# Block-recurrent cross attention and an ELU layer on one core: planner costs for loads and stores, longer runs for moved softmax weights, and two softmax steps on GpSimd

## The chip, the cores and the metric

The kernel runs on one core of a Trainium2 chip. The metric is the device time of one execution in microseconds, the median of the runs. Names: PE is the matrix engine (PEld its weight loads), DVE or VectorE the vector engine, ACT or ScalarE the scalar engine, POOL or GpSimd the fourth compute engine, SP the engine whose queue issues nearly all DMAs. SBUF and PSUM are the on-chip memories[...].

## The reference

```python
B, H, S, Ns, D = 8, 8, 512, 32, 64        # x: (B,H,S,D), state: (B,H,Ns,D)
scores = x @ state.T / sqrt(D);  a = softmax(scores)      # over the 32 states
xread  = a @ state                                        # (B,H,512,64)
scores2 = state @ x.T / sqrt(D); a2 = softmax(scores2)    # over the 512 rows
sread  = a2 @ x                                           # (B,H,32,64)
t = concat([xread, sread], axis=2)        # 544 rows per batch
t = t.transpose(0, 2, 1, 3).reshape(4352, 512)
h = t @ w_in                              # 512 -> 2048
g = where(h > 0, h, exp(min(h, 0)) - 1)   # ELU
out = g @ w_out                           # 2048 -> 512
```

All is in float32.

## The kernel before

**Work by batch.** The 512 x rows of a batch never pass through xread. The kernel multiplies the state of the batch with w_in first (`make_m`, four pieces, PSUM to the tiles m or s by ScalarE), so that the first layer is a product of these pieces with the softmax a, held transposed in the tile aT (`a_sb`). Both layers use a seven-product scheme (Strassen with Winograd's sums), so every product needs sums of blocks: the sums of the m pieces and of a_sb run on GpSimd (`sum_m`, `sum_a`), those of the second layer on VectorE (`Second.sums`, `combine`). sread is collected for all batches (`state_read`) and goes through both layers at the end (`states`).

**One batch in the steady loop** (`batch(b)`, b = 2 to 7):

- `load_blocks(b+1, ob)`: 16 DMAs of 64 KB bring the next x, in 128 B runs, into the tile o. The same tile holds the finished output rows of the batch before until `store` has written them out, so these loads follow the stores.
- The first layer: four chunks (`ffn1_chunk`) of seven products of two matmuls of 128x128 by 128x256. ScalarE and VectorE take each result from PSUM: copies into u2 and u3 (tile sec), additions back into PSUM (`ps<-sec,ps`), the ELU (`xe`, then `g`).
- `turn_blocks(ob, xr)`: four VectorE transposes in 32x32 blocks (`xr<-o`), one for each group of four block loads.
- The second layer (`ffn2`): one product of 16 pairs of matmuls, then six sub-products of seven steps each (`second[2]`, `[4]`, `[6]`, `[7]`, `[5]`, `[3]`). Each step's result is added to the output tile by VectorE (`o<-o,ps`). Near its start come `scores(b+1)` into two PSUM banks of their own (6 and 7) from xr.
- `soft_next()` inside `ffn2`, for the next batch: `softmax` (over states) into a_sb, `softmax_rows` (over rows), `load_x` (four DMAs of 256 KB into xe), `move_state` and then the GpSimd sums. a_sb is also scratch for the sums of `second[2]` and `second[6]`, so the new softmax can be written to it only when `second[6]` has been multiplied.
- `state_read(b+1)`, near the end of `ffn2`: needs xe and the moved weights.

**softmax(b, to)** for a half g, on tiles of 128x512: transpose from PSUM to xr (VectorE), maximum over 32 (VectorE), subtract it (`xr<-xr,small`), exp (ScalarE), sum (VectorE); then, for both halves, reciprocal (VectorE), multiply (`xr<-xr,small`), transpose into a_sb (VectorE). The subtraction and the multiplication have two tile operands. For b > 1 they are on VectorE, for b = 0 and 1 on GpSimd.

**move_state(b)**: two VectorE transposes put the row softmax back into the first half of xr, then 16 DMAs of 32 KB move it to the second half of xr, 32 partitions each, in 8 runs of 128 B per partition. `turn_state` does this for batches 0 and 1 by PE and a ScalarE copy.

**Order.** Every operation is recorded in a `Plan` with a cost; `Plan.order` runs a list scheduler over them three times and keeps the best order. All engines then execute their instructions in that order, each in its own. PE's operations are preferred in the order of the program, those of VectorE, ScalarE and SP by due time, GpSimd's stay in program order. For a DMA, `DMA_COST` gives the issue cost and the rate; the plan adds `LANDING` = 2.2 us. `plan.behind(op)` makes the operations recorded inside it (GpSimd's excepted) depend on `op` in the plan; it puts no wait into the program. In `ffn2` the list `late` collects such marks: `late[4]` is the last sum of `second[6].sums`, `late[6]` the last one of `second[7].sums`.

Because all instructions are emitted by one helper (line 463), the profile shows L463 everywhere; groups are told apart by tile names: xr<-o are `turn_blocks`, o<-in_x_dram `load_blocks`, xr<-xr DMAs `move_state`, aT `a_sb`.

Of the kernel before, what the change touches and what calls it, by code (L numbers as in the profile page):

```python
# [21 lines left out]
ENGINES = (POOL, PE, DVE, ACT, SP)  # L22
DMA_COST = {
    "load_w": (0.44, 285e3), "load_w4": (0.44, 370e3), "load_x": (0.6, 270e3), "load_states": (0.6, 75e3),
    "load_blocks": (0.66, 280e3), "move_state": (0.66, 280e3),
}


# [50 lines left out]
class Op:  # L79
    __slots__ = (  # L80
        "number", "engine", "cost", "emit", "deps", "opens", "closes", "port", "moved", "start",
        "end", "due", "users", "name", "instr", "shape", "rank", "rate", "turn", "nudge", "spare",
    )


class Plan:
# [51 lines left out]
    def add(self, engine, cost, emit, ins, outs, port=False, moved=0, tokens=((), ()), name="", shape=None):  # L138
        op = Op()
        op.number, op.engine, op.cost, op.emit = len(self.ops), engine, cost, emit  # L140
        op.deps, op.opens, op.closes, op.port, op.moved = set(), None, [], port, moved
        op.name, op.shape, op.rank, op.rate = name, shape, None, 350e3
        op.nudge, op.spare = 0.0, None
        pieces = []
        banks = {}
        for writes, aps in ((False, ins), (True, outs)):
            for a in aps:
                if isinstance(a, View):
                    banks[id(a.bank)] = a.bank
                else:  # L150
                    pieces.append((writes,) + self.region(a))
        for writes, names in enumerate(tokens):
            for t in names:
                self.writers.setdefault(t, [])
                self.readers.setdefault(t, [])
                pieces.append((bool(writes), t, 1))
        for writes, key, mask in pieces:
            if key is None:
                continue
            for m, o in self.writers[key]:  # L160
                if m & mask:
                    op.deps.add(o)
            if writes:
                for m, o in self.readers[key]:
                    if m & mask:
                        op.deps.add(o)
        for writes, key, mask in pieces:
            if key is None:
                continue
            if writes:  # L170
                self.writers[key] = [
                    (m & ~mask, o) for m, o in self.writers[key] if m & ~mask
                ] + [(mask, op)]
                self.readers[key] = [(m & ~mask, o) for m, o in self.readers[key] if m & ~mask]
            else:
                self.readers[key].append((mask, op))
        for b in banks.values():
            if b.last is None:
                b.first = op
            else:  # L180
                op.deps.add(b.last)
            b.last = op
        op.deps.discard(op)
        self.ops.append(op)
        return op
# [52 lines left out]
    def run(self, until=0.0):  # L238
# [68 lines left out]
        while len(done) < len(self.ops):  # L307
            best = None
            for e in ENGINES:
                found = pick(e)  # L310
                if found and (best is None or found[0] < best[0] - 1e-9):
                    best = found + (e,)
            assert best is not None, "no operation is ready"
            at, op, e = best
            if e == POOL:
                in_turn.pop(0)
            able[e].remove(((op.turn if e == PE else op.due), op.number, op))
            if e == PE:
                t = free_at[PE]
                while at < until and t + 0.5 < at:  # L320
                    free = [i for u, i in banks if u <= t]
                    if free:
                        fills.append((t, free[-1], 0))
                    elif spare:
                        fills.append((t, spare.index, 1))
                    t += 0.3
            for bank in self.opening.get(op, ()):
                t, i = got = choice(op)[0]
                banks.remove(got)
                bank.index = i  # L330
                if i in holder:
                    after.append((holder[i], op))
                opened.add(op)
            if op in self.kept:
                banks = [b for b in banks if b[1] != self.kept[op]]
                if self.kept[op] in holder:
                    after.append((holder[self.kept[op]], op))
            while oldest < len(openers) and openers[oldest] in opened:
                oldest += 1
            if e == PE and (op.spare or op.name == "make_m"):  # L340
                spare = op.spare
            if e == PE and op.shape != shape:
                at += self.TURN
                shape = op.shape
            op.start, op.end = at, at + op.cost
            free_at[e] = op.end
            if op.port:
                port, holds = op.end, e
            if op.moved:
                wire = max(wire, op.end) + op.moved / op.rate  # L350
                op.end = wire + self.LANDING
                lanes.append(op.end)
            done.append(op)
            for u in op.users:
                ready[u] = max(ready[u], op.end + self.lag(op, u))
                waiting[u] -= 1
                if not waiting[u]:
                    release(u)
            for b in self.closing.get(op, ()):
                bisect.insort(banks, (op.end + self.LAG[op.engine].get(PE, 0.0), b.index))  # L360
                holder[b.index] = op
# [27 lines left out]
def kernel(  # L389
# [154 lines left out]
    def dma(out, in_, tokens=((), ()), queue=SP, kind="dma"):  # L544
        size = 4 * elements(out) * out.shape[0]
        engine = nc.sync if queue == SP else nc.scalar
        cost, rate = DMA_COST.get(kind, (0.44, 370e3))
        op = plan.add(
            queue, cost, issue(engine, "dma_start", dict(out=out, in_=in_)), [in_], [out],
            moved=size, tokens=tokens, name=kind,  # L550
        )
        op.rate = rate

    def bank():
        return Bank(plan).view()
# [194 lines left out]
    def softmax(b, to):  # L750
# [7 lines left out]
            V.transpose(out=soft_t(b, g), in_=s[g])  # L758
        for g in range(G):
            V.reduce_max(out=tops(b, g)["top_t"], in_=rows(g), axis=AX_X)  # L760
            (V if 3 & 1 and b > 1 or b in [] else Q).tensor_tensor(
                out=rows(g), in0=rows(g), in1=bc(tops(b, g)["top_t"], NS), op=ALU.subtract
            )
            A.activation(out=soft_t(b, g), in_=soft_t(b, g), func=AF.Exp, scale=scale)
            V.reduce_sum(out=tops(b, g)["total_t"], in_=rows(g), axis=AX_X)
        V.tensor_scalar(out=total_t, in0=total_t, scalar1=eps, scalar2=None, op0=ALU.add)
        V.reciprocal(out=total_t, in_=total_t)
        for g in range(G):
            (V if 3 & 2 and b > 1 or b in [] else Q).tensor_tensor(
                out=rows(g), in0=rows(g), in1=bc(tops(b, g)["total_t"], NS), op=ALU.mult  # L770
            )
            V.transpose(out=to[:, g * 512 : (g + 1) * 512], in_=soft_t(b, g))

    def read_weights():
        return xr[:, 1024:].rearrange("p (g r q) -> p g r q", g=G, q=P)

    def turn_state(b):
        for g in range(G):
            ps = bank().rearrange("p (r q) -> p r q", r=R)
            a = soft_a(b, g).rearrange("p (r q) -> p r q", r=R)  # L780
            turns(0.6, [(ps[:, r], a[:, r], ident, {}) for r in range(R)], "turn_state")
            A.copy(out=read_weights()[:, g], in_=ps)

    def move_state(b):
        t = xr[:, :1024]
        for g in range(G):
            V.transpose(out=t[:, g * 512 : (g + 1) * 512], in_=soft_a(b, g))
        t_v = t.rearrange("p (g r q n) -> p g r q n", g=G, r=R, n=NS)
        for m in range(NP):
            for q in range(P // 32):  # L790
                dma(
                    read_weights()[q * 32 : (q + 1) * 32, :, :, m * NS : (m + 1) * NS],
                    t_v[m * 32 : (m + 1) * 32, :, :, q], kind="move_state",
                )

    def state_read(b, at=x_halves):
        ps = bank()
        calls = []
        for g in range(G):
            for r in range(R):  # L800
                for m in range(NP):
                    calls.append((
                        ps[m * NS : (m + 1) * NS, g * D : (g + 1) * D],
                        read_weights()[:, g, r, m * NS : (m + 1) * NS],
                        x_rows(at, r)[:, m * P + g * D : m * P + (g + 1) * D],
                        dict(start=r == 0, stop=r == R - 1, tile_position=(0, m * NS)),
                    ))
# [260 lines left out]
    def store(b, h, o):  # L1068
        rows = out_b[b, 0:S].rearrange("(p r) c -> p r c", r=R)
        dma(rows[:, 2 * h : 2 * h + 2], o.o_sb[h], kind="store")  # L1070

    def words(raw):
        return [raw.rearrange("p n (j w) -> p n j w", w=2)[:, :, :, i] for i in range(2)]
# [196 lines left out]
    def ffn2(o, b):  # L1270
# [42 lines left out]

        def soft_next():
            if nxt:
                with plan.behind(late[4]):
                    softmax(b + 1, a_sb)
                    softmax_rows(b + 1)
                    load_x(b + 1, x_halves)
# [297 lines left out]
```

## Time and profile before

| | |
|---|---|
| median of 3 runs | 712.54 us (711.35 to 713.09) |
| the profiled execution | 712.58 us, span 710.7 us |
| PE busy | 695.2 us, 98% |
| VectorE busy | 584.5 us, 82% |
| ScalarE busy | 304.9 us, 43% |
| GpSimd busy | 113.8 us, 16% |
| DMA | 132771 packets, 78.54 MB; 113760 packets under 512 B |

The span is the time from the first to the last instruction of one profiled execution; the time of an execution includes about 1.9 us around it. Matmuls overlap and the profile models their ends, so stalls of PE are better read from the distance between the starts of consecutive matmuls: 0.216 us for 128x128 by 128x256 in an unbroken row, 0.112 us for 128x128 by 128x128. A bracket at the end of a timeline row is the engine's idle time before it and what ended it.

### The profile page before, as it was taken

What the parts mean: (1) busy time and instruction counts of PE and PEld (TensorE: products, weight loads), DVE (VectorE), ACT (ScalarE), POOL (GpSimd) and SP (SyncE); (2) the same over time, 40 slices, a digit from 0 to 9 for tenths busy, and PEclk for the clock granted to TensorE, in tenths of its full rate; (3) what the DMA queues carried; (4) which work ended last, traced back from release to release, by engine and by line L of the source; (5) the groups of instructions that cost most, each with busy time, mean ns of one, the idle gap of its engine ahead of it and who ended that gap; (6) DMA issues with size and microseconds to landing.
All of it is one profiled execution on the core that took longest, in us unless ns stands there. A gap on an engine that the chain in (4) does not pass through costs nothing.

```text
span 710.7 us, 14531 instructions
## 1 busy us (share of the span) xinstructions
PE 695.2 (98%) x5802; PEld 589.9 (83%) x5802; DVE 584.5 (82%) x1039; ACT 304.9 (43%) x604; POOL 113.8 (16%) x137
## 2 busy tenths in 40 slices
PE   8899999999999999999999999999999999999996
PEld 7544478889978998789877997799878988899995
DVE  4989999999659996799679994899579976997640
ACT  4989981011066124731275124712374127500630
POOL 1400000022230034100710063002510063000000
PEclk9999999999999999999999999999999999999999
DMA  9677772214270416550482326340664035200300
GB/s 221 197 265 244 272 241 44 59 36 114 90 193 15 120 32 187 110 119 2 93 231 64 61 50 187 91 120 3 186 141 115 5 64 205 60 1 31 119 8 24
DMA packets 132771, 78.54 MB, mean 111 GB/s; under 512 B 113760, under 2 KB 114272, under 8 KB 132704
## 3 DMA queue, kind: packets, MB, share of 16 engines
q1 hardware_dynamic: 130492, 77.06, 39.6%
q8 instruction: 46, 0.75, 0.4%
q10 hardware_dynamic: 2212, 0.56, 0.4%
q14 instruction: 21, 0.17, 0.1%
HBM read 61.34 MB, written 13.11 MB: 105 GB/s over the span
## 4 chain that ended last, share of the span: by engine, by line
PE 82%; DMA 6%; SPq 5%; ACT 2%; DVE 2%; issue 1%; ACTq 0%; DVEq 0%
PE ps L463 82%; SPq L463 5%; DMA w_in_mem<-w_half 2%; DMA o<-in_x_dram 2%; DMA out_dram<-o 1%; DVE g L463 1%; ACT sec L463 1%; DMA xe<-in_x_dram 1%; DMA g<-in_x_dram 1%; DVE ps L463 1%; ACT w_half L463 0%; ACT xe L463 0%; DVE xr L463 0%; ACT o L463 0%; ACTq L463 0%
## 5 line engine op out<-in xcount | busy, mean ns | idle before, releaser
L463 PE MATMUL ps<-aT,m 128*128 128x256 f32 (+1 forms) x568 | 151.2, 408 | 3.6 <-DVE ps L463 1.3
L463 PE MATMUL ps<-w_out,g 128*128 128x128 f32 (+1 forms) x864 | 143.5, 314 | 0.0
L463 PEld LDWEIGHTS ps<-w_out,g 128*128 128x128 f32 x864 | 126.3, 191 | 12.7 <-issue 4.2
L463 PEld LDWEIGHTS ps<-aT,m 128*128 128x128 f32 x568 | 104.2, 190 | 35.7 <-issue 15.9
L463 DVE TENSOR_TENSOR o<-o,ps 128x128 f32<-128x128 f32 (+2 forms) x239 | 67.4, 283 | 43.1 <-PE ps L463 41.5
L463 ACT COPY o<-ps 128x128 f32<-128x128 f32 (+2 forms) x70 | 23.1, 335 | 170.3 <-PE ps L463 164.3
L463 POOL TENSOR_TENSOR m<-m 128x256 f32<-128x256 f32 x72 | 65.9, 939 | 76.6 <-ACT m L463 75.2
L463 POOL TENSOR_TENSOR aT<-aT 128x256 f32<-128x256 f32 x24 | 17.9, 767 | 361.6 <-DVE aT L463 361.2
L463 PE MATMUL ps<-sec 128*128 128x128 f32 x560 | 74.8, 276 | 0.0
L463 ACT ACTIVATE xe<-ps 128x512 f32<-128x512 f32 x96 | 56.2, 597 | 38.5 <-DVE ps L463 21.5
L463 PEld LDWEIGHTS ps<-sec 128*128 128x128 f32 x560 | 68.1, 192 | 2.6 <-DVE sec L463 2.1
L463 PE MATMUL ps<-t_w,s 128*128 128x128 f32 (+1 forms) x432 | 64.7, 299 | 0.0
L463 PEld LDWEIGHTS ps<-t_w,s 128*128 128x128 f32 x432 | 58.4, 192 | 3.7 <-ACT m L463 0.8
L463 DVE SCALAR_TENSOR_TENSOR g<-xe,ps 128x512 f32<-128x512 f32 x66 | 43.9, 681 | 16.2 <-ACT xe L463 16.0
L463 ACT COPY m<-ps 128x512 f32<-128x512 f32 (+1 forms) x56 | 27.1, 534 | 59.6 <-PE ps L463 59.6
L463 PE MATMUL ps<-aT,s 128*128 128x256 f32 x168 | 41.8, 383 | 2.6 <-DVE ps L463 2.4
L463 ACT COPY sec<-ps 128x512 f32<-128x512 f32 (+1 forms) x52 | 29.6, 570 | 30.9 <-PE ps L463 17.4
L463 ACT ACTIVATE xe<-xe 128x512 f32<-128x512 f32 x66 | 40.7, 632 | 1.2
L463 PEld LDWEIGHTS ps<-aT,s 128*128 128x128 f32 x168 | 31.2, 190 | 9.4 <-DVE ps L463 4.0
L463 PE MATMUL ps<-w_half,kT 64*32 64x256 f32 x1024 | 35.9, 382 | 1.5 <-DVE w_half L463 0.9
L463 DVE TENSOR_TENSOR ps<-sec,ps 128x512 f32<-128x512 f32 (+1 forms) x52 | 34.7, 667 | 2.0 <-ACT sec L463 1.0
L463 ACT COPY ps<-ps 128x512 f32<-128x512 f32 (+1 forms) x28 | 15.3, 547 | 45.7 <-PE ps L463 45.7
(152 smaller groups left out, 1147.0 us busy)
## 6 DMA issues: line engine op xcount, KB each, us to landing
w_half<-w_in_mem SPq DMA_DIRECT2D x54, 512.0 KB
t_w<-in_moe_w_out_dram SPq DMA_DIRECT2D x8, 1024.0 KB
t_w<-in_moe_w_in_dram SPq DMA_DIRECT2D x7, 1024.0 KB
out_dram<-o SPq DMA_DIRECT2D x14, 512.0 KB
xe<-in_x_dram SPq DMA_DIRECT2D x26, 256.0 KB
o<-in_x_dram SPq DMA_DIRECT2D x80, 64.0 KB
w_in_mem<-w_half SPq DMA_DIRECT2D x8, 512.0 KB
xr<-xr SPq DMA_DIRECT2D x96, 32.0 KB
```

The lines of the kernel that those rows point to most:

```text
L463: ins = getattr(engine, name)(**named)
```

## The change

Four things are changed.

1. Costs in the planner: a block load lands 1.5 us later in the plan (field `wait`), and a store has its own rate of 200e3 bytes per us where the default was 370e3.
2. `softmax`: the subtraction and the multiplication go to GpSimd for every batch.
3. The state weights: their place in xr is ordered by (m, g, r, n), so that each of the 16 DMAs of `move_state` moves one run of 1 KB per partition; the transposes in front of them and the copies of `turn_state` write to strided places, and `state_read` reads the new order. The amounts are the same.
4. `soft_next` is planned behind `late[6]`.

The line `nudge = 0` sets the value that is there already.

```diff
 DMA_COST = {
 ...
-    "load_blocks": (0.66, 280e3), "move_state": (0.66, 280e3),
+    "load_blocks": (0.66, 280e3, 1.5), "move_state": (0.66, 280e3),
+    "store": (0.44, 200e3),
 }
...
                 wire = max(wire, op.end) + op.moved / op.rate
-                op.end = wire + self.LANDING
+                op.end = wire + self.LANDING + op.wait
...
-        cost, rate = DMA_COST.get(kind, (0.44, 370e3))
+        cost, rate, *wait = DMA_COST.get(kind, (0.44, 370e3))
...
-        op.rate = rate
+        op.rate, op.wait = rate, sum(wait)
...
-            (V if 3 & 1 and b > 1 or b in [] else Q).tensor_tensor(
+            (V if 0 & 1 and b > 1 or b in [] else Q).tensor_tensor(
                 out=rows(g), in0=rows(g), in1=bc(tops(b, g)["top_t"], NS), op=ALU.subtract
             )
...
-            (V if 3 & 2 and b > 1 or b in [] else Q).tensor_tensor(
+            (V if 0 & 2 and b > 1 or b in [] else Q).tensor_tensor(
                 out=rows(g), in0=rows(g), in1=bc(tops(b, g)["total_t"], NS), op=ALU.mult
             )
...
     def read_weights():
-        return xr[:, 1024:].rearrange("p (g r q) -> p g r q", g=G, q=P)
+        return xr[:, 1024:].rearrange("p (m g r n) -> p m g r n", m=NP, g=G, n=NS)
...
-            A.copy(out=read_weights()[:, g], in_=ps)
+            A.copy(
+                out=read_weights()[:, :, g].rearrange("p m r n -> p r m n"),
+                in_=ps.rearrange("p r (m n) -> p r m n", n=NS),
+            )
 
     def move_state(b):
-        t = xr[:, :1024]
+        t = xr[:, :1024].rearrange("p (q g r n) -> p g r q n", g=G, r=R, n=NS)
         for g in range(G):
-            V.transpose(out=t[:, g * 512 : (g + 1) * 512], in_=soft_a(b, g))
-        t_v = t.rearrange("p (g r q n) -> p g r q n", g=G, r=R, n=NS)
+            V.transpose(
+                out=t[:, g], in_=soft_a(b, g).rearrange("p (r q n) -> p r q n", r=R, n=NS)
+            )
         for m in range(NP):
             for q in range(P // 32):
                 dma(
-                    read_weights()[q * 32 : (q + 1) * 32, :, :, m * NS : (m + 1) * NS],
-                    t_v[m * 32 : (m + 1) * 32, :, :, q], kind="move_state",
+                    xr[q * 32 : (q + 1) * 32, 1024 + m * 256 : 1280 + m * 256],
+                    xr[m * 32 : (m + 1) * 32, q * 256 : (q + 1) * 256], kind="move_state",
                 )
...
-                        read_weights()[:, g, r, m * NS : (m + 1) * NS],
+                        read_weights()[:, m, g, r],
...
         dma(rows[:, 2 * h : 2 * h + 2], o.o_sb[h], kind="store")
+        plan.ops[-1].nudge = 0
...
-                with plan.behind(late[4]):
+                with plan.behind(late[6]):
                     softmax(b + 1, a_sb)
```

More of the change, by code (lines that the diff above doesn't have):

```diff
@@ L81 @@
         "number", "engine", "cost", "emit", "deps", "opens", "closes", "port", "moved", "start",
-        "end", "due", "users", "name", "instr", "shape", "rank", "rate", "turn", "nudge", "spare",
+        "end", "due", "users", "name", "instr", "shape", "rank", "rate", "turn", "nudge", "spare", "wait",
     )
@@ L142, in add @@
         op.name, op.shape, op.rank, op.rate = name, shape, None, 350e3
-        op.nudge, op.spare = 0.0, None
+        op.nudge, op.spare, op.wait = 0.0, None, 0.0
         pieces = []
```

## The prediction

> **What bounds the kernel now.** I read the page's busy table first. The matrix unit is hardly ever idle, so a gain can only be a gap between its matmuls.
>
> ```profile
> span 710.7 us, 14531 instructions
> ...
> PE 695.2 (98%) x5802; PEld 589.9 (83%) x5802; DVE 584.5 (82%) x1039; ACT 304.9 (43%) x604; POOL 113.8 (16%) x137
> ```
>
> Next, the list of waits: which of them end at PE, and what holds VectorE, whose products PE waits for.
>
> ```profile
> DVE xr L463 <- DMA o<-in_x_dram: 14.1, 13, 5.2
> ...
> PE ps L463 <- DVE ps L463: 3.7, 6, 1.0
> ```
>
> VectorE stands still 14.1 us, in 13 pieces, in front of the block transposes of the next batch (xr<-o), which wait for the block loads. PE's longest waits are for VectorE's writes into PSUM. The timeline at one of them, the first block of batch 5:
>
> ```profile
> 442.30 1.03 PE L463 MATMUL ps<-aT,m 128*128 128x256 f32 x4
> 443.00 0.71 DVE L463 STREAM_TRANSPOSE xr<-o 128x512 f32<-128x512 f32 x1 [2.40 <-DMA o<-in_x_dram]
> 443.64 0.67 DVE L463 TENSOR_TENSOR ps<-sec,ps 128x512 f32<-128x512 f32 x1
> 444.36 0.91 PE L463 MATMUL ps<-aT,m 128*128 128x256 f32 x3 [1.03 <-DVE ps L463]
> ```
>
> VectorE waits 2.40 us for a load, transposes, and only then makes the addition that PE wants. Such matmuls start every 0.216 us, so the fourth of the first group began at 442.95; the next came at 444.36: 1.41 - 0.22 = 1.20 us lost. I summed, over the first layer of every batch, the spacings above the steady one that end at VectorE, or at a ScalarE copy that stood behind VectorE: 0.47 (batch 2, at 210.6), 1.45 (batch 3, 291 to 300), 1.62 (batch 4, 372 and 377), 1.93 (batch 5, 443 to 451), 1.41 us (batch 6, 528 and 534). **Sum 6.9 us.** Batch 7 loads no next x, and there PE has no such gap (596 to 640 us). The batch period agrees: scores to scores takes 77.68, 77.70, 78.31 and 77.49 us; less the four last losses, 76.1 to 76.4 each. Other gaps (about 0.3 us at each 32-row product) and the start are not touched.
>
> **What the Trainium skill says.** (1) "SBUF — State Buffer", on concurrent engine access: a VectorE instruction with two SBUF inputs and a GpSimd instruction that reads SBUF exclude each other. The trace agrees that they cost each other: in the POOL and VectorE timelines of batch 4,
>
> ```profile
> 415.23 2.93 POOL L463 TENSOR_TENSOR aT<-aT 128x256 f32<-128x256 f32 x4 [49.05 <-DVE aT L463]
> 418.11 8.34 POOL L463 TENSOR_TENSOR m<-m 128x256 f32<-128x256 f32 x8
> ```
>
> four GpSimd steps beside transposes and PSUM additions take 2.93 us (0.73 each), eight beside sums take 8.34 (1.04 each), and those sums grow from 0.68 to 1.2 us.
> (2) "GPSIMD Engine Reference", Performance versus the Vector engine: a two-input step takes about twice as long there. Trace: 1308 ns against 684 ns (rows below), 1.91 times.
> (3) "DMA: Bandwidth & Descriptors", why small descriptors are slow: small runs hurt with HBM, much less from SBUF to SBUF. The trace fits: while the state weights are moved in 128 B runs (424.2 to 429 us) the DMA engines are busy only 0.30 of the time.
>
> **The change part by part.**
>
> ```profile
> L463 POOL TENSOR_TENSOR sec<-sec 128x512 f32<-128x512 f32 x8 | 10.3, 1308 | 24.8 <-DVE sec L463 24.8
> L463 DVE TENSOR_TENSOR xr<-xr,small 128x512 f32<-128x512 f32 x24 | 16.3, 684 | 0.0
> ```
>
> *Costs of loads and stores in the planner.* Nothing on the chip changes but the order. A store's 512 KB goes from 524288/370e3 = 1.42 us to 524288/200e3 = 2.62, so the block loads, which write the stored tile, are planned 1.2 us later; each is planned to land 1.5 us later. The four transposes become ready 2.7 us later in the plan and stand behind some four more VectorE steps. The measured wait is 14.1/5 = 2.8 us per batch, and the chain of waits shows the store taking 6.25 us from issue where the plan had 0.44 + 1.42 + 2.2 = 4.1. So the correction has the right size. The elementwise steps and PSUM additions then run inside the wait. What is late next: the transposes go into 375 to 385 us, where VectorE works without a pause, and push the sums there by 4 x 0.71 = 2.8 us less the wait saved, 2.8: nothing. The scores that read them start at 386.7, 11.7 us after the last ended. The queue of SP keeps its loads; fetches may pass them, at 0.4 us each, hidden by those 11.7 us. Worth 0 to 6.9 us. The planner's order cannot be exact (the waits differ by batch, from 0.1 to 5.2 us), so I take 80%: **-5.5 us**.
>
> *Softmax steps to GpSimd.* 24 steps (four for each of six batches) leave VectorE: 24 x 0.684 = 16.4 us. They cost GpSimd 24 x 1.308 = 31.4, which has 597 free. Contention: in 418 to 426 us six VectorE sums lost some 2.6 us beside 8.3 us of GpSimd; four steps of 1.31 to about 2 us stretch VectorE by 1.6 to 2.6 us per batch, where it saved 2.7. VectorE gains 0 to 1 us per batch, at a place where PE does not wait for it: **0 us**. The chain gets longer: 4 x (1.31 - 0.68) = 2.5 us, contended 4 x (2.0 - 0.68) = 5.3. In VectorE's order the reductions and transposes of softmax wait for these steps, and the PSUM additions behind them would wait too.
>
> *Softmax behind late[6].* It starts after the sums for the seventh sub-product, not the sixth: after 401.65 instead of 397.1 in batch 4, 4.5 us later. Its loads (4 of x, 16 of state weights) come after it in the plan only; on the chip SP issues what is ready. The old chain rests between the sum's end at 406.46 and the reciprocal at 412.50: 6.0 us. So a_sb comes later by 4.5 + 2.5 - 6.0 = 1.0 us, contended 4.5 + 5.3 - 6.0 = 3.8. Who waits: GpSimd's 12 sums (415.2 to 426.5), then the first products of the next batch (422.07). PE has work without them: 1.05 + 0.97 + 3.57 = 5.6 us of make_m and second layer after 423.9. That covers 3.8: **0 us**, and each us beyond 5.6 would cost PE one in each of five batches.
>
> *State weights in 1 KB runs.* 96 loads x 256 runs of 128 B become 96 x 32 of 1 KB. The issue sets the pace (0.609 us each, 16 in a row), not the wires. No row shows the new shape: the issue rows go from 0.32 (one long run per partition) to 0.61 us, so SP gains 0 to 16 x 0.29 = 4.6 us per batch; I take 0.5 us. state_read (431.31) waits for the last of them, issued to 428.94; softmax's 1.0 to 3.8 us delay is met by that gain and by products of the next batch. The transposes in front write 32-element pieces at strides; no row shows that. 12 of them at 0.68: between nothing and a doubling, 8 us on VectorE in all, at a place with pauses. Copies of turn_state: four, in the start, likewise. **0 us.**
>
> Sum: 712.58 (the profiled execution: span 710.7 plus 1.9 around it) - 5.5 = 707.1. The median of the runs is 712.54, 0.04 lower, so **707.0 us**.
>
> **The rivals.** A difference under 0.3% (2.1 us) cannot be told from none here.
> *Half of it.* The transposes move too little, or VectorE now stands in front of reductions and transposes that wait for GpSimd (0.3 us later than its planned 1.01 at each of four steps, 1.2 us per batch, five batches: 6 us, part of it before PE). Gain 0 to 3.4: 709.1 to 712.5. For it: 1308 ns against the plan's 1.01 us. Against: the 6 us rest in the chain.
> *Slower: a_sb late.* If the order leaves no rest in the chain (other sums stay ahead of the reciprocal), the delay is 4.5 + 2.5 = 7.0 to 9.8 us and PE stops once it passes 5.6 us: 1.4 to 4.2 us in each of five batches, 7 to 21 us, less the 5.5 gained: 714 to 728, likeliest 718. The place: the first products with a_sb after each second layer. Against: the reciprocal rests by the planner's choice, not for a resource.
> *Nothing happens.* The transposes' order comes from due times as well; if these keep it, 712.5.
>
> **How the numbers follow.** Forecast (gain 3.4 to 8, 704.5 to 709.1): 0.62. Half: 0.2, two thirds of it beyond 0.3%. Nothing: 0.05. Late a_sb: 0.13. Faster 0.62 + 0.13 = 0.75; same 0.07 + 0.05 + 0.01 = 0.13; slower 0.12. The low end 704.0 is all 6.9 us and 1.6 more from a luckier order; the high end 714.0 takes in the half and the nothing and the start of the late case.
>
> **What would show it.** Right: VectorE's wait for o<-in_x_dram falls from 14.1 us below 4; PE's waits for VectorE's PSUM writes in the first layers nearly vanish; the period falls to about 76.4 us; VectorE loses 16 us, GpSimd gains 31 to 45; packets under 512 B fall by 24576. Wrong: PE waits at products with aT after the second layer or at state_read; VectorE waiting for POOL xr in the softmax with PE behind it; transposes still waiting over 2 us per batch.

## The result, and the profile after

The changed kernel takes 705.71 us, the median of its runs, against 712.82 us for the kernel before beside it: ratio 0.9903, interval 0.9875 to 0.9932. It is faster by about 1%. All medians here are of fast runs: two executions, one of the changed kernel (1016 us, at a granted clock of 0.66) and one of the kernel before (1443 us), are left out as far slower than the rest. The profiled execution took 707.31 us with a span of 705.5 us; a second profile of the same kernel (run 5 below) had a span of 703.6 us. Of the 1.9 us between them 1.1 lie in the start, before the scores of batch 2; the rest lies in batches 3 and 4.

The page's busy table, to be set beside the one in the prediction (the helper that emits all instructions stands at line 464 here, so L464 stands for what was L463):

```profile
span 705.5 us, 14564 instructions
...
PE 692.4 (98%) x5802; PEld 591.9 (84%) x5802; DVE 577.5 (82%) x1015; ACT 301.3 (43%) x604; POOL 139.4 (20%) x161
```

VectorE has 24 instructions fewer (1039 to 1015) but only 7 us less busy time, not the 16.4 us that they took: the others have become longer. The list of waits, PE's part after and one line of before:

```profile
PE ps L464 <- DVE o L464: 3.7, 8, 0.6
...
PE ps L464 <- ACT kT L464: 1.1, 1, 1.1
```

```profile
PE ps L463 <- DVE o L463: 0.3, 1, 0.3
```

PE's 3.7 us of waits for VectorE's writes into PSUM (`DVE ps`) are gone from the list. In their place stand 3.7 us for VectorE's additions to the output tile (`DVE o`), which were 0.3 us before. The groups of instructions (busy us, mean ns, idle us before them and what ended it), after and then before:

```profile
L464 POOL TENSOR_TENSOR xr<-xr,small 128x512 f32<-128x512 f32 x24 | 26.9, 1140 | 306.9 <-PE ps L464 156.9 <-DVE small L464 150.0
...
L464 DVE STREAM_TRANSPOSE xr<-o 128x512 f32<-128x512 f32 x20 | 14.0, 702 | 0.0
...
L464 DVE TENSOR_SCALAR small<-small 128x2 f32<-128x2 f32 x12 | 7.5, 625 | 0.0
```

```profile
L463 DVE STREAM_TRANSPOSE xr<-o 128x512 f32<-128x512 f32 x20 | 14.1, 708 | 14.4 <-DMA o<-in_x_dram 14.1
L463 DVE TENSOR_SCALAR small<-small 128x2 f32<-128x2 f32 x12 | 1.9, 158 | 0.0
```

The block transposes wait for nothing: idle before them 0.0, where it was 14.4 us. GpSimd's softmax steps are there, at 1140 ns. And an instruction on two elements per partition takes 625 ns in the mean, where it took 158 before. The place where that happens is the second layer of every batch; here batch 4, first VectorE, then GpSimd (both multiplications in one row, then the first alone, in a narrower window), then PE in the timeline:

```profile
411.07 1.01 DVE L464 TENSOR_SCALAR small<-small 128x2 f32<-128x2 f32 x1
411.99 0.27 DVE L464 TENSOR_TENSOR o<-o,ps 128x128 f32<-128x128 f32 x1
412.19 1.42 DVE L464 TENSOR_TENSOR sec<-g 128x512 f32<-128x512 f32 x1
413.53 0.27 DVE L464 TENSOR_TENSOR o<-o,ps 128x128 f32<-128x128 f32 x1
```

```profile
410.75 2.31 POOL L464 TENSOR_TENSOR xr<-xr,small 128x512 f32<-128x512 f32 x2 [7.69 <-DVE small L464]
```

```profile
410.75 1.30 POOL L464 TENSOR_TENSOR xr<-xr,small 128x512 f32<-128x512 f32 x1 [7.69 <-DVE small L464]
```

```profile
412.18 1.06 PE L464 MATMUL ps<-sec 128*128 128x128 f32 x8
413.86 0.38 PE L464 MATMUL ps<-t_w,s 128*128 128x128 f32 x1 [0.62 <-DVE o L464]
```

While GpSimd multiplies (410.75 to 413.06), VectorE's two-element step takes 1.01 us and the sum sec<-g 1.42 us (0.68 elsewhere). Both end as if held until a GpSimd step was over: the first multiplication ends at 412.05 and the two-element step at 412.08; the second ends at 413.06 and the sum 0.55 us later, at 413.61. The addition o<-o,ps behind the sum is late by 0.85 + 0.74 = 1.59 us, and PE, which needs its PSUM bank read, starts 0.78 us late by the spacing of its matmuls. So some 0.8 us of the delay were slack. This recurs in the five batches 2 to 6: 3.9 us.

The period from scores to scores is 76.40, 76.86, 76.91 and 76.40 us (before: 77.68, 77.70, 78.31, 77.49). In the two longer ones, of batches 3 and 4, a second two-element step is held as well, and PE loses a further 0.34 us. In batch 4 that step and the GpSimd step beside it, a sum with which it shares no tile, are

```profile
414.53 0.73 DVE L464 TENSOR_SCALAR small<-small 128x2 f32<-128x2 f32 x1
```

```profile
414.50 0.72 POOL L464 TENSOR_TENSOR aT<-aT 128x256 f32<-128x256 f32 x1 [1.45 <-DVE aT L464]
```

In the second profile this step is not held in any batch.

### The profile page after: what moved, and what is told of

It is laid out like the page before. It is cut to its first block, busy times and chain, and to the rows that moved or that the text cites. A ratio compares the mean times of both kernels' runs of the same rounds, so it can differ in the third digit from the quotient of the medians.

```text
span 705.5 us, 14564 instructions
## 1 busy us (share of the span) xinstructions
PE 692.4 (98%) x5802; PEld 591.9 (84%) x5802; DVE 577.5 (82%) x1015; ACT 301.3 (43%) x604; POOL 139.4 (20%) x161
## 2 busy tenths in 40 slices
DMA packets 111268, 78.55 MB, mean 111 GB/s; under 512 B 89184, under 2 KB 92768, under 8 KB 111200
## 4 chain that ended last, share of the span: by engine, by line
PE 82%; DVE 12%; DMA 2%; issue 2%; ACT 1%; SPq 1%; ACTq 0%; DVEq 0%
PE ps L464 82%; DVE small L464 3%; DVE o L464 3%; DVE sec L464 2%; DVE s L464 2%; DMA xe<-in_x_dram 1%; DVE g L464 1%; DMA g<-in_x_dram 1%; SPq L464 1%; DVE xr L464 0%; DVE aT L464 0%; PE ps L1581 0%; ACT sec L464 0%; ACT t_w L464 0%; ACTq L464 0%
## 5 line engine op out<-in xcount | busy, mean ns | idle before, releaser
L464 PE MATMUL ps<-aT,m 128*128 128x256 f32 (+1 forms) x568 | 148.8, 406 | 1.1 <-ACT kT L464 1.1
L464 PE MATMUL ps<-w_out,g 128*128 128x128 f32 (+1 forms) x864 | 144.5, 315 | 0.0
L464 PEld LDWEIGHTS ps<-w_out,g 128*128 128x128 f32 x864 | 126.6, 191 | 14.7 <-issue 6.2
L464 PEld LDWEIGHTS ps<-aT,m 128*128 128x128 f32 x568 | 105.1, 190 | 29.1 <-issue 13.1
L464 DVE TENSOR_TENSOR o<-o,ps 128x128 f32<-128x128 f32 (+2 forms) x239 | 66.6, 282 | 50.0 <-PE ps L464 48.5
L464 ACT COPY o<-ps 128x128 f32<-128x128 f32 (+2 forms) x70 | 23.2, 335 | 153.5 <-PE ps L464 153.5
L464 POOL TENSOR_TENSOR xr<-xr,small 128x512 f32<-128x512 f32 x24 | 26.9, 1140 | 306.9 <-PE ps L464 156.9
L464 POOL TENSOR_TENSOR m<-m 128x256 f32<-128x256 f32 x72 | 65.9, 937 | 70.8 <-ACT m L464 69.4
L464 PE MATMUL ps<-sec 128*128 128x128 f32 x560 | 74.0, 275 | 0.0
L464 PEld LDWEIGHTS ps<-sec 128*128 128x128 f32 x560 | 68.4, 192 | 0.4
L464 PE MATMUL ps<-t_w,s 128*128 128x128 f32 (+1 forms) x432 | 65.1, 300 | 3.1 <-DVE o L464 3.1
L464 PEld LDWEIGHTS ps<-t_w,s 128*128 128x128 f32 x432 | 58.4, 191 | 7.3 <-DVE o L464 4.1
L464 ACT ACTIVATE xe<-ps 128x512 f32<-128x512 f32 x96 | 55.5, 600 | 19.5 <-DVE ps L464 12.8
L464 ACT COPY m<-ps 128x512 f32<-128x512 f32 (+1 forms) x56 | 27.1, 535 | 71.8 <-PE ps L464 71.7
L464 ACT COPY sec<-ps 128x512 f32<-128x512 f32 (+1 forms) x52 | 29.8, 574 | 46.0 <-PE ps L464 45.9
L464 DVE SCALAR_TENSOR_TENSOR g<-xe,ps 128x512 f32<-128x512 f32 x66 | 43.7, 679 | 1.2 <-ACT xe L464 1.2
L464 DVE TENSOR_SCALAR xe<-xe 128x512 f32<-128x512 f32 x30 | 15.7, 527 | 31.2 <-ACT xe L464 26.1
L464 PE MATMUL ps<-aT,s 128*128 128x256 f32 x168 | 40.9, 382 | 0.0
L464 ACT ACTIVATE xe<-xe 128x512 f32<-128x512 f32 x66 | 40.0, 637 | 0.9
L464 DVE TENSOR_TENSOR ps<-sec,ps 128x512 f32<-128x512 f32 (+1 forms) x52 | 34.8, 669 | 5.7 <-PE ps L464 4.2
L464 PEld LDWEIGHTS ps<-aT,s 128*128 128x128 f32 x168 | 31.3, 190 | 6.4 <-issue 2.1
L464 PE MATMUL ps<-w_half,kT 64*32 64x256 f32 x1024 | 35.0, 382 | 0.0
```

Of the source, the lines that this page charges most:

```text
L464: ins = getattr(engine, name)(**named)
```

## The experiments

All ratios are to the kernel before in the same set of runs, with 95% intervals. The median of the kernel before moved from 712.3 to 714.9 us between the sets; medians of two kernels are set against each other directly only within a set, or where it is said.

**1. The wait alone.** The order of before is kept to the instruction on VectorE; only the loads are missing.

```diff
                     kind="load_blocks",
                 )
+                if b > 2:
+                    plan.ops[-1].emit = lambda: None
```

> The kernel before, in its own order, with the block loads of batches 3 to 7 left out (the transposes then read what the tile holds, so the numbers are not the reference's). Theory (VectorE standing in front of the transposes for the loads is what PE loses): 712.8 - 6.9 = about 706 us, VectorE's wait for o<-in_x_dram gone, PE's gaps in the first layers gone. Rival (the wait is hidden and PE's gaps come from VectorE's load itself): 711 to 713 us, the gaps stay.

Measured: 702.49 us, ratio 0.9843 (0.9815 to 0.9871). In the groups of this kernel:

```profile
L463 DVE STREAM_TRANSPOSE xr<-o 128x512 f32<-128x512 f32 x20 | 13.9, 700 | 0.0
```

The theory holds and its size was too small: not 6.9 us but some 11 in the medians, 8.0 between the two spans (710.7 and 702.7). The periods say where: 75.99, 75.66, 76.78 and 75.66 us (the third holds a wait of 1.06 us for xr<-xr). In the two periods of before that I took apart, the spacings in excess of the steady one by 0.03 to 0.25 us sum to 3.9 and 4.2 us a batch, here to 3.4 to 3.5. The wait had also produced 0.4 to 0.7 us per batch in delays too small for my count of 6.9. The loads' own traffic is absent here too, so the next run is the cleaner price.

**2. The planner costs alone**, on the kernel before:

```diff
-    "load_blocks": (0.66, 280e3), "move_state": (0.66, 280e3),
+    "load_blocks": (0.66, 280e3, 1.5), "move_state": (0.66, 280e3),
+    "store": (0.44, 200e3),
```

> The kernel before with the two planner costs alone (block loads land 1.5 us later, stores at 200e3). Theory (the later transposes carry the whole gain): 706 to 708 us, VectorE's wait for o<-in_x_dram under 2 us. Rival (the softmax parts are needed too, since the transposes only move the crowd on VectorE elsewhere): 709 to 713 us, with new PE gaps in the second layer.

Measured: 702.76 us, ratio 0.9842 (0.9814 to 0.9869), span 700.3 us. Groups:

```profile
L464 DVE STREAM_TRANSPOSE xr<-o 128x512 f32<-128x512 f32 x20 | 13.8, 702 | 0.0
```

The rival falls. The costs carry more than the whole gain of the change, and the three other parts together give some of it back. The periods are 75.58, 75.59, 75.59 and 75.80 us.

**3. The change without the planner costs:**

```diff
-    "load_blocks": (0.66, 280e3, 1.5), "move_state": (0.66, 280e3),
-    "store": (0.44, 200e3),
+    "load_blocks": (0.66, 280e3), "move_state": (0.66, 280e3),
```

> The changed kernel with the two planner costs as they were before. Theory (later transposes carry the gain): back to 711 to 714 us, VectorE's wait for o<-in_x_dram back at 10 to 15 us. Rival (GpSimd's softmax steps and late[6] carry it): 705 to 708 us.

Measured: 711.69 us, ratio 0.9974 (0.9961 to 0.9988). The wait is back, in the groups of this kernel:

```profile
L463 DVE STREAM_TRANSPOSE xr<-o 128x512 f32<-128x512 f32 x20 | 14.2, 710 | 13.8 <-DMA o<-in_x_dram 13.4 <-issue 0.3
```

So undoing this part undoes nearly all of the gain.

**4. The 1 KB runs alone**, on the kernel before (`read_weights`, `turn_state`, `move_state` and `state_read` as in the change, nothing else):

> The kernel before with the state weights moved in 1 KB runs, nothing else. Theory: no difference, 711.5 to 713.5 us, 24576 packets of under 512 B fewer, the 16 issues at 0.3 to 0.6 us each. Rival (the moves hold up state_read or crowd the fetches): 708 to 711 us.

Measured: 710.35 us, ratio 0.9952 (0.9929 to 0.9974). This is a small gain where I expected none; the time lies in the rival's range, though the trace does not show the rival's reason (state_read starts as long after the scores as before). The issue of a move takes 588 ns in the median (609 before), as expected. VectorE's order is nearly that of before, and the groups show the wait for the block loads a little shorter:

```profile
L463 DVE STREAM_TRANSPOSE xr<-o 128x512 f32<-128x512 f32 x20 | 14.1, 709 | 13.8 <-DMA o<-in_x_dram 13.5
```

Three of the four periods are shorter by 0.1 to 0.6 us and one is longer by 0.1: 1.0 us in all, of some 3.5 us between the medians. Why the wait is shorter stays open. The moves and the block loads do not meet on the wires: the last move is issued about 42 us after the scores, the first block load about 50 us after them. That first load comes 0.2 to 0.3 us earlier than before in three of the five batches and not in the other two. If the gain lies in this wait at all, then the runs must gain nothing where the transposes don't wait; run 8 tests that.

**5. The changed kernel again**, as the yardstick of the next three:

> The changed kernel once more, as the yardstick of this set: 705 to 707 us, PE's losses of 0.78 us in the second layer of five batches (in front of the matmuls with t_w and s) as in its first profile.

Measured: 705.57 us, ratio 0.9871 (0.9847 to 0.9896), the losses 0.78 us in each of five batches, periods 76.45, 76.43, 76.40 and 76.40 us.

**6. The multiplication left out**, in the changed kernel's own order:

```diff
                 out=rows(g), in0=rows(g), in1=bc(tops(b, g)["total_t"], NS), op=ALU.mult
             )
+            if b > 1:
+                plan.ops[-1].emit = lambda: None
```

> The changed kernel in its own order, with softmax's multiplication left out for batches 2 to 7 (the weights are then not normalised). Theory (GpSimd's multiplication holds the port that VectorE's sum wants, so the PSUM addition behind that sum is late and PE loses 0.78 us a batch): about 4 us less than the changed kernel, 701 to 703 us, the loss gone. Rival (the loss comes from the order, a sum standing in front of the addition, whoever holds the port): no difference, 705 to 707 us.

Measured: 701.92 us, ratio 0.9825 (0.98 to 0.985): 3.7 us less than run 5 of the same set, for about 4 forecast. VectorE's order is the same to the instruction, and its timeline at the same place (batch 4) shows the sum at its own length and the addition waiting for PE, not PE for it:

```profile
410.12 0.68 DVE L464 TENSOR_TENSOR sec<-g 128x512 f32<-128x512 f32 x1
411.17 0.29 DVE L464 TENSOR_TENSOR o<-o,ps 128x128 f32<-128x128 f32 x1 [0.37 <-PE ps L464]
```

PE has no loss left there; the periods are 75.73 to 75.74 us. The rival (the order, whoever holds the port) falls. "The port" is the access to SBUF from which, by the first point of the prediction, the two engines exclude each other; what the traces show of it is that VectorE's steps do not end before GpSimd's.

**7. The multiplication on VectorE in the same order.** It is planned as a GpSimd step and executed by VectorE:

```diff
+            if b > 1:
+                plan.ops[-1].emit = issue(nc.vector, "tensor_tensor", dict(
+                    out=rows(g), in0=rows(g), in1=bc(tops(b, g)["total_t"], NS), op=ALU.mult
+                ))
```

> The changed kernel in its own order, with the multiplication executed by VectorE at the place where the plan has it on GpSimd. Theory (what GpSimd takes from VectorE by holding the port, 1.5 us a batch, is as much as the 2 x 0.68 us it saves it): the same time as the changed kernel within 1.5 us, the losses in the same place. Rival (the port's conflict costs more than the work): 3 to 4 us less.

Measured: 703.98 us, ratio 0.9846 (0.9822 to 0.987), 1.6 us less than run 5. Neither forecast was quite met. VectorE's timeline in batch 4:

```profile
409.06 0.68 DVE L464 TENSOR_TENSOR xr<-xr,small 128x512 f32<-128x512 f32 x1
409.65 0.16 DVE L464 TENSOR_SCALAR small<-small 128x2 f32<-128x2 f32 x1
409.73 0.28 DVE L464 TENSOR_TENSOR o<-o,ps 128x128 f32<-128x128 f32 x1
409.92 0.68 DVE L464 TENSOR_TENSOR sec<-g 128x512 f32<-128x512 f32 x1
410.52 0.68 DVE L464 TENSOR_TENSOR xr<-xr,small 128x512 f32<-128x512 f32 x1
411.13 0.28 DVE L464 TENSOR_TENSOR o<-o,ps 128x128 f32<-128x128 f32 x1
```

Both multiplications now stand in front of the addition, one before the two-element step and one behind the sum, and PE loses 0.39 us per batch, half of 0.78. By the starts of what follows, they delay the addition by 0.59 + 0.61 = 1.20 us; as GpSimd's steps they delayed it by 1.59. The difference, 0.39 us, is what PE loses less, so the same 0.8 us of slack stand in both runs. The totals for VectorE are nearly alike, as I had said.

**8. Costs and 1 KB runs**, with softmax on VectorE and behind late[4] (the change without its GpSimd and late[6] lines):

> The kernel before with the planner costs and the 1 KB runs, softmax on VectorE and behind late[4]. Theory (of the four parts only the costs and, by 1 to 3 us, the runs gain; GpSimd's steps and late[6] give some of it back): 700 to 702.5 us, faster than the changed kernel by 3 to 6 us. Rival (the parts belong together): 704 to 707 us.

Measured: 702.87 us, ratio 0.9837 (0.981 to 0.9863), 2.7 us less than run 5, a little under the forecast of 3 to 6; the time itself lies between the two forecasts. It stands beside 702.76 and 0.9842 of the costs alone, and its periods of 75.58, 75.59, 75.67 and 75.59 us are those of run 2 within 0.2: where the transposes don't wait, the runs gain nothing. The theory's "by 1 to 3 us, the runs" was wrong.

**9. The block loads' 1.5 us without the store's rate:**

> The kernel before with the block loads planned to land 1.5 us later, the store's rate left alone. Theory (the shift has to cover the measured wait of 2.8 us a batch, and this is 1.5 of it): about half the gain, 705 to 709 us, VectorE's wait for o<-in_x_dram at 4 to 9 us. Rival (any shift past the next elementwise steps is enough): 702 to 704 us, the wait under 2 us.

Measured: 703.82 us, ratio 0.9882 (0.9861 to 0.9902); VectorE's wait for the block loads 0.4 us in all. The rival was right: 1.5 us moves the transposes behind enough other steps, except in batch 3, where PE still loses 0.64 us behind one (period 76.39, the others 75.59 to 75.82). By the periods of the two runs, the store's rate is worth 0.8 us in four batches; the medians of different sets don't resolve it.

**10. Both softmax steps on VectorE, the rest as in the change, planned anew:**

```diff
-            (V if 0 & 1 and b > 1 or b in [] else Q).tensor_tensor(
+            (V if 3 & 1 and b > 1 or b in [] else Q).tensor_tensor(
...
-            (V if 0 & 2 and b > 1 or b in [] else Q).tensor_tensor(
+            (V if 3 & 2 and b > 1 or b in [] else Q).tensor_tensor(
```

> The changed kernel with both softmax steps back on VectorE (costs, 1 KB runs and late[6] stay), planned anew. Theory (the multiplication on GpSimd is all that the change gives back, late[6] costs nothing): 702 to 704 us, no loss of over 0.5 us in the second layers. Rival (softmax behind late[6] comes too late): 704.5 to 708 us, PE waiting at products with aT or at state_read.

Measured: 701.46 us, ratio 0.9851 (0.9829 to 0.9873), a little below the theory's range. Its page:

```profile
span 699.7 us, 14535 instructions
...
PE 690.0 (99%) x5802; PEld 590.7 (84%) x5802; DVE 579.6 (83%) x1039; ACT 301.8 (43%) x604; POOL 109.9 (16%) x137
```

VectorE has its 24 instructions back and is busy 2.1 us longer than in the changed kernel; all four periods are 75.57 us, where run 8, which differs only in late[4], has 75.58 to 75.67. So late[6] costs nothing in this version. This version beats both kernels: its slowest run, 703.1 us, is below the fastest of the changed kernel in either set, 704.82.

**11. The change with late[4] for late[6], planned anew:**

> The changed kernel with softmax behind late[4] again (costs, 1 KB runs and GpSimd stay), planned anew. Theory (the multiplication on GpSimd costs in this order too, wherever it meets a two-input sum): 704.5 to 707 us. Rival (the loss is an accident of the order with late[6]): 702 to 704 us.

Measured: 703.90 us, ratio 0.9881 (0.9861 to 0.9901). This is at the upper end of the rival's range: a loss of 0.53 us for `o<-o,ps` in batches 2, 4 and 6 and none over 0.25 us in batches 3 and 5 (periods 76.44, 75.79, 76.43, 75.77). In batch 4 the multiplication holds only the two-element step, by 0.2 us; the larger stretch is that of a sum of VectorE's, 1.62 us (1.22 in batch 5), beside GpSimd's next step, a sum of a_sb:

```profile
404.78 0.36 DVE L464 TENSOR_SCALAR small<-small 128x2 f32<-128x2 f32 x1
...
405.25 1.62 DVE L464 TENSOR_TENSOR s<-s,g 128x1024 f32<-128x1024 f32 x1
```

```profile
405.07 0.72 POOL L464 TENSOR_TENSOR aT<-aT 128x256 f32<-128x256 f32 x1
```

What a GpSimd step costs depends on what stands beside it on VectorE, and so on the order.

**12. The multiplication on VectorE, the subtraction on GpSimd, planned anew** (the second line of run 10's diff alone):

> The changed kernel with the multiplication on VectorE and the subtraction on GpSimd, planned anew. Theory (the subtraction has a rest behind it and costs nothing there): 702 to 704 us. Rival (any two-input step on GpSimd in the second layer costs): 704.5 to 707 us.

Measured: 701.89 us, ratio 0.9851 (0.9828 to 0.9875), no loss over 0.25 us outside the start. The periods are 75.69, 75.92, 75.69 and 75.69 us, 0.1 to 0.35 above those of run 10. The subtraction can stay on GpSimd at next to no cost, and with no gain.

## Why the prediction was right, and which terms were wrong

The time (705.71 for 707.0 us), the sign and the likeliest case came out. The path to them did so in part: two terms of the sum were wrong in opposite directions and nearly cancelled, so that the time came this near is luck.

- **What bounded the kernel: right.** PE's losses came from VectorE standing in front of the transposes (runs 1 to 3), and the transposes moved as the costs said. VectorE's wait went from 14.1 us to nothing, below the 4 us named. The last transpose now ends 69.4 to 69.9 us after the scores, with 7 us to spare before the next.
- **The term of -5.5 us for the planner costs was too small.** It rested on 6.9 us of spacings above a quarter of a microsecond, of which I took 80%. By the periods, the costs alone (run 2) saved 2.10, 2.11, 2.72 and 1.69 us, 8.6 us in four batches; by the medians, 1.58% or some 11 us. What was missing is the small delays: in these four periods the counted spacings fell by 6.1 us and those of 0.03 to 0.25 us (4.0 a batch before, 3.4 in run 2) by 2.6, which makes up the 8.6. My check by the periods had a hole: I subtracted the counted losses and took the rest (76.1 to 76.4 us) for the floor, but it is 75.6.
- **The term of 0 us for GpSimd was wrong: it costs 3.7 us** (run 6), all of it by the multiplication (run 12). The sizes in it were nearly right: a step took 1.14 us (1.31 priced), and VectorE lost 1.6 us per batch to the softmax steps (1.6 to 2.6 forecast), where it was rid of 2.7. The step that failed is "at a place where PE does not wait for it". In before PE did not wait there; but the additions `o<-o,ps` that release PSUM banks stand behind the stretched steps, and they had some 0.8 us of slack for a delay of 1.6. The rival "half of it" had VectorE wait for GpSimd's results; that happens once, for 1.2 us. The planner does keep GpSimd's steps apart in time from VectorE's steps with two tile operands and from its large copies and tensor_scalars (`port`), but it takes 1.01 us for a multiplication, which took 1.30 and 1.04 us, and its rule leaves out operands of four elements or fewer, so the two-element step is free to stand beside one. That these two errors made the loss is likely, but no run corrects them.
- **Softmax behind late[6] at 0 us: right.** a_sb comes 1.8 us later after the scores, 2.4 in two batches (1.0 to 3.8 forecast), state_read 2.4 us later, 2.9 in two, without PE waiting; the rest in the chain took it up, and run 10 shows the same for VectorE's version. The rival "a_sb late" did not occur.
- **The 1 KB runs at 0 us: right inside the change** (run 8 beside run 2), though not in the kernel before (run 4). Packets under 512 B fell from 113760 to 89184, by the 24576 forecast. The issue fell to 588 ns, not to the 0.5 us I took. The transposes that write at strides took 676 ns (680 before), so that doubt was empty.
- **The marks** set for the changed profile: the period of about 76.4 us came out to the digit, by luck, as the sum of the two errors: 75.6 for the order plus 0.8 for GpSimd's multiplication. VectorE's busy time fell by 7.0 us where 16 were set, since other steps were stretched, and GpSimd's rose by 25.6 where 31 to 45 were.

## What to carry to other kernels

An in-order engine that waits for a load holds up everything behind it. Its waits and the gaps seen elsewhere enclosed the price here: 14.1 us of waiting cost PE 8 to 11 us, of which gaps over 0.25 us showed 6.9; counting the small gaps too closed the account. Telling the planner a later landing time, nearer to the measured one, repaired it without changing a single operation. When work goes to an engine beside which another's steps grow longer, look not only at the sum but at the instructions behind those that will be stretched, and ask who needs them within the stretch.

## What the runs showed of the hardware

- A VectorE tensor_scalar on two elements per partition can be held by a GpSimd step: 625 ns on average over all twelve (528 in the second profile), 158 before. Beside the first multiplication it took 1.01 us and ended within 0.03 us of it, in each of five batches of both profiles. Beside a sum of GpSimd's that had begun only 0.02 to 0.03 us earlier it was held in two of ten cases; in run 6, where that sum had begun 0.11 us earlier, in all five. I had counted only steps with two tile operands. The Trainium skill, "SBUF — State Buffer", Who interferes with whom, lists tensor_scalar among the instructions that can take the shared pair; the runs agree, down to this size.
- In these conflicts VectorE bore most of the loss: two multiplications took GpSimd 2.31 us, where the two subtractions of the same shape took 2.05 in the same batch, while VectorE's two steps grew by 1.6 us. The first multiplication took 1.30 us and began while a sum of VectorE's ran, the second 1.04.
- A move with one run of 1 KB per partition took 588 ns to issue (median), where 8 runs of 128 B took 609: in these moves the count of runs hardly sets the price.
